# Weight conversion in three program stages instead of two, and the feature tiles of the scores' PSUM place first

## The chip, the cores and the metric

The kernel runs on one core of one Trainium2 chip. The metric is the device time of one execution in microseconds (us). The kernel before takes 1092.17 us, the median of three runs (1091.16 to 1093.48).

## The reference

An attention over chunks of 64 tokens feeds an FNet block. Batch 8, 8 heads, 576 tokens, head size 64, so the model size is 512; the feed-forward width is 2048.

```python
scores = scale * q_c @ k_c.T          # per batch, head and chunk of 64 tokens
attn   = softmax(scores)
x      = (attn @ v_c) -> (8, 576, 512)
u      = x + real(fft(fft(x, axis=1), axis=2))
un     = (u - mean(u)) / sqrt(var(u) + 1e-6)
out    = u + relu(un @ w_ch1) @ w_ch2
```

The two weights arrive as 64-bit floats. The kernel turns them into 32-bit floats itself, and that conversion is what the change is about.

## The kernel before

**Groups and sides.** Tokens are gathered in tiles of 128 rows. Group g of the feed-forward layer holds four such tiles (512 columns); group 0 belongs to batch 0, group 1 to batch 1, and so on. While TensorE multiplies for group g, the attention and the Fourier mix of batch g + 1, called its side, are worked in between. The main loop (lines 1213 to 1247) takes one step of `mlp(g)`, counts it in `t`, and then emits as many steps of the side as are due (`t0`, `t1`, `due`, lines 1218 to 1220). The order is written out by hand: under `manual_schedule` each engine, and the queue of the DMA issues on SyncE (SPq), works its instructions in the order in which the program emits them.

**Group 0.** `up_first` (line 943) has four blocks of four feature tiles (f = 0, 4, 8, 12) and four steps kk in each; step (f, kk) needs weight piece f + kk of `w_ch1`. A step is 8 matmul records of 128x512. At the end of a block ScalarE evicts four tiles (lines 962 and 965). The sixteen steps m of `down_plain` (line 988) follow; step m needs piece 16 + m, a slice of `w_ch2`. The first block's four tiles, `first_ups`, are two tiles of the pool `ps_f` and two halves of the one buffer of `ps_a` (tag "att"). The attention scores `sc` (line 379) and the attention outputs use this same `ps_a` buffer.

**Weight pieces.** There are 32 pieces of 128x512 numbers (`pieces`, line 266), 512 KB each as they arrive. `round_weight(i)` does for piece i the head h(i): two VectorE instructions that cut out the fraction and the exponent (lines 308 and 311); then the three ScalarE activations a(i) (lines 300, 303 and 306); and then the tail t(i - 1) of the piece before: three VectorE instructions (lines 321 to 323) that put the number together. One call is thus h(i), a(i), t(i - 1). Calls are made by `round_next`, once or twice in a step of the main loop (lines 1229 to 1231), none in a step in which the side did heavy VectorE work.

**Landing places.** A piece lands in one of seven spaces (`spaces`, line 138; numbered 0 to 6). A tail gives its space back and lets `load_weight` (line 279) issue the next load. Pieces from 8 on may use spaces 0 to 4 only (`N_EARLY`, `N_LATE`); pieces from 26 on (`N_LAST`) may use 2, 3 and 4 only, since spaces 0 and 1 are wanted by `keep2`, which prepares `w_ch2` for the later groups on VectorE once all pieces are converted.

**The side of batch 1.** `attention` (line 569) and `fourier` (line 644). The steps that the prediction names: T(n) transposes q and k of the side's tile n and issues the loads of the next tile; S(n) is the scores and, on VectorE, the maximum and the difference (lines 397 and 399), then the exponential on ScalarE; P(n) transposes the probabilities (`pT`, line 416); V(n) multiplies with v and divides on VectorE (lines 454 to 456). V(2) and V(3) also fold the tiles on VectorE (lines 491 to 529): these are the heavy steps. T(4) is the first tile of batch 2 and is transposed on VectorE (line 352). Then come z (line 652), its copies on ScalarE (lines 677 to 688), and three `mix` steps (line 700), each followed by VectorE (lines 710, 711, 717, 637). The normalised tile `un` (line 843) of group 1 needs the last of these.

Of the kernel before, what the change touches and what calls it, by code (L numbers as in the profile page):

```python
# [10 lines left out]
ACTF = mybir.ActivationFunctionType  # L11
# [5 lines left out]
def kernel(  # L17
# [32 lines left out]
    nc = tc.nc  # L50
# [9 lines left out]
    KD = DM // 128  # L60
    KF = DFF // 128
# [194 lines left out]
    def turn_dim_tables():  # L256
# [9 lines left out]
    pieces = [  # L266
        (w1[:, kk, f:f + 512], w_ch1[kk * 128:(kk + 1) * 128, f:f + 512])
        for f in range(0, DFF, 512)
        for kk in range(KD)
    ] + [(w2[:, m, :], w_ch2[m * 128:(m + 1) * 128, :]) for m in range(KF)]  # L270

    power = {}

    raws, free = {}, list(range(len(spaces)))

# [11 lines left out]
    def round_weight(i, later=None, parts="ht"):  # L287

        if "h" in parts and i < len(pieces):
            w, t = pieces[i][0], raw(i)
            lo, hi, wi = t[:, :, 0], t[:, :, 1], w.bitcast(U32)
            p = power[i] = three_p.tile([128, 512], U32, tag="o", name="power")

            def fraction(w=w, wi=wi):
                nc.scalar.activation(out=w, in_=wi, func=ACTF.Copy, scale=2.0 ** -20, bias=1.0)  # L300

            def exponent(p=p):
                nc.scalar.activation(out=p, in_=p, func=ACTF.Relu, scale=-1.0, bias=top[:, 0:1])

            def power_(p=p):
                nc.scalar.activation(out=p, in_=p, func=ACTF.Relu, scale=-8.0, bias=top[:, 1:2])

            nc.vector.tensor_scalar(wi, hi, 0x000FFFFF, None, ALU.bitwise_and)
            if later is None:
                fraction()  # L310
            nc.vector.tensor_scalar(p, hi, 0x7FF00000, None, ALU.bitwise_and)
            if later is None:
                exponent()
                power_()
            else:
                later += [fraction, exponent, power_]
        if "t" in parts and 0 < i <= len(pieces):
            w, t = pieces[i - 1][0], raw(i - 1)
            lo, hi = t[:, :, 0], t[:, :, 1]
            p = power.pop(i - 1)  # L320
            nc.vector.scalar_tensor_tensor(w, lo, 2.0 ** -52, w, ALU.mult, ALU.add)
            nc.vector.scalar_tensor_tensor(p, hi, 0x80000000, p, ALU.bitwise_and, ALU.bitwise_or)
            nc.vector.tensor_tensor(out=w, in0=w, in1=p.bitcast(FP32), op=ALU.mult)
            r = raws.pop(i - 1)
            if i - 1 + len(spaces) < N_EARLY or r < N_LATE:
                free.append(r)
            load_weight(max(raws, default=i - 1) + 1)
# [203 lines left out]
    def attention_early():  # L531

        lo, hi = first[0], first[1] - 1

        def ready(n):
            if n == at[LO, 0, 1]:
                shift_early(0)
            if n == at[HI, 0, 1]:
                fold(0, 1)
            if n == at[HI, 0, 0]:  # L540
                fold(0, 0)
            if n + 3 > hi:
                load_v(n + 3)

        att_T(lo)
        att_S(lo)
        for n in range(lo, hi + 1):
            if n < hi:
                att_T(n + 1)
            softmax(n)  # L550
            if n > lo:
                att_V(n - 1)
                ready(n - 1)
            if n < hi:
                att_S(n + 1)
            if n in (lo, hi):
                keep_warm(1)
            att_P(n)
        shift_early(1)
        fold(0, NM)  # L560
        keep_warm(1)
        att_V(hi)
        ready(hi)
        keep_warm(6)
        turn_tables()
        round_weight(0)
        round_weight(1, parts="t")

    def attention(b):

# [156 lines left out]
    def fourier_early():  # L727
# [53 lines left out]
        keep_warm(3)  # L781
        yield
        ups = ps_a.tile([128, 2, 512], FP32, tag="att", name="up_a")
        first_ups.extend([ps_f.tile([128, 512], FP32, tag="ff", name="up") for _ in range(2)])
        first_ups.extend([ups[:, i] for i in range(2)])

        def columns(s):

# [154 lines left out]
    def up_first():  # L943

        unT = unTs.pop(0)
        h1 = one_p.tile([128, KF, G * 128], FP32, tag="big", name="h1")
        for f in range(0, KF, 4):
            ups = first_ups if f == 0 else [ps_f.tile([128, G * 128], FP32, tag="ff", name="up") for _ in range(4)]  # L950
            for kk in range(KD):
                for m, up in enumerate(ups, f) if f + kk > 0 else ():
                    nc.tensor.matmul(  # L953
                        out=up,
                        lhsT=w1[:, kk, m * 128:(m + 1) * 128],
                        rhs=unT[:, kk],
                        start=(kk == 0),
                        stop=(kk == KD - 1),
                        skip_group_check=True,
                    )  # L960
                    if kk == KD - 1 and (f > 0 or m < 2):
                        nc.scalar.activation(out=h1[:, m], in_=up, func=ACTF.Relu)  # L962
                if kk == KD - 1 and f == 0:
                    for m in (2, 3):
                        nc.scalar.activation(out=h1[:, m], in_=ups[m], func=ACTF.Relu)
                yield h1

    def up_plain(g):
# [19 lines left out]
    def down_plain(g, h1):  # L988

        dns = [ps_f.tile([128, 512], FP32, tag="ff", name="dn") for _ in groups[g]]
        for m in range(KF):
            for s, dn in enumerate(dns):
                nc.tensor.matmul(  # L995
                    out=dn,
                    lhsT=h1[:, m, s * 128:(s + 1) * 128],
                    rhs=w2[:, m, :],
                    start=(m == 0),
                    stop=(m == KF - 1),  # L1000
                )
                if m == KF - 1:
                    n = groups[g][s]
                    if s < G - 1:
                        o = three_p.tile([128, DM], FP32, tag="o", name="o")
                    else:
                        o = one_p.tile([128, 2 * (HM + 1)], FP32, tag="two", name="o")[:, 0:DM]
                    nc.vector.tensor_tensor(out=o, in0=dn, in1=natural(n), op=ALU.add)
                    store(n, o)
            for j in range(G):  # L1010
                due = KF - (G - j + 1)
                if m == due - 2:
                    normed(g + 1, j)
                if m == due:
                    turned(g + 1, j)
                    if j >= 2 and g + 1 >= first_of[1]:
                        combined(g + 1, j - 2)
            yield
# [121 lines left out]
    with tc.manual_schedule():  # L1140
# [20 lines left out]
        n_w = 2  # L1161
# [8 lines left out]
        put_off, first_ups = [], []  # L1170

        def round_next(later=None):
            nonlocal n_w
            if n_w <= len(pieces):
                round_weight(n_w, later)
                n_w += 1

        keep_warm(8)
        attention_early()
# [32 lines left out]
        t = 0  # L1212
        for g in range(NG):
            for _ in mlp(g):
                t += 1
                heavy = False
                if cur < len(sides):
                    t0 = 2 if cur == 0 else ready_at[cur - 1]
                    t1 = ready_at[cur]
                    due = min(sizes[cur], (t - t0) * sizes[cur] // (t1 - t0))  # L1220
                    while done < due:
                        heavy = next(sides[cur], None) or heavy
                        done += 1
                    if t >= t1:
                        for _ in sides[cur]:
                            pass
                        cur, done = cur + 1, 0
                if not heavy:
                    round_next()
                    if t <= 1 or t < KF and t % 4 == 0 or t >= KF + 3:  # L1230
                        round_next()

                if n_w > len(pieces) and t >= KF + 7:
                    for _ in range(3):
                        next(conv2, None)
                if t == begin[1] - 1:
                    for _ in conv2:
                        pass
                if begin[1] <= t < begin[1] + KF // 2:
                    for _ in range(3):  # L1240
                        next(conv1, None)
                if t == begin[1] + KF // 2:
                    for _ in range(NS2):
                        fetch(2)
                if t == begin[1] + KF:
                    for _ in range(NS1):
                        fetch(1)
# [49 lines left out]
```

## Time and profile before

| what | value |
|---|---|
| time, median of 3 | 1092.17 us |
| span of the profiled execution | 1090.8 us |
| TensorE busy (modelled) | 1069.5 us |
| VectorE busy | 576.9 us |
| ScalarE busy | 298.8 us |
| mean granted TensorE clock | 0.999 |
| group 0, up and down | about 46 to 190 us of the span |
| conversion of pieces 2 to 31 | about 48 to 156.5 us of the span |

Busy time is a sum over the whole span. The stage of the change is only a seventh of it, so the views to read are those that can be cut to a stretch: the busy time by stretch, the timeline of one engine (start, duration, instruction, and in brackets the idle time before it with what ended it), and the chain that ended last in order of time.

### The profile page before, as it was taken

To read this page: it belongs to the slowest core of one execution; us is meant where nothing else is said; L and a number is where in the kernel's file an instruction comes from. 1 tells how busy PE (TensorE), PEld (TensorE's weight loads), DVE (VectorE), ACT (ScalarE), POOL (GpSimd) and SP (SyncE) were. 2 spreads that over 40 slices of the span, in tenths; PEclk is the share of its full clock that TensorE was granted. 3 is DMA by queue.
4 is the path that set the end of the run, shared out by engine and by line. 5 is a ranking of instruction groups with operands and counts; after the bars stand their busy time and mean duration, and the time that the engine had idled before them with its cause. 6 is when DMAs were issued, how large, how long until landed. Compare 5 with 4: busy or idle time off the path is not lost.

```text
span 1090.8 us, 18838 instructions
## 1 busy us (share of the span) xinstructions
PE 1069.5 (98%) x7018; PEld 848.3 (78%) x7018; DVE 576.9 (53%) x1258; ACT 298.8 (27%) x730; POOL 281.4 (26%) x403
## 2 busy tenths in 40 slices
PE   8999999999999999999999999999999999999998
PEld 6644454447888888888888888888888888888887
DVE  4889997214566355663556455735663534323411
ACT  4777553222112310322022212321133103101300
POOL 4300002344405240254024220514051401220140
PEclk9999999999999999999999999999999999999999
DMA  8767656679575637692668457754653455446232
GB/s 170 243 168 180 174 169 227 176 239 307 177 204 165 198 135 205 196 263 89 197 170 228 140 169 221 203 175 150 198 184 89 143 196 160 122 154 210 78 116 78
DMA packets 147970, 192.73 MB, mean 177 GB/s; under 512 B 66126, under 2 KB 104014, under 8 KB 140712
## 3 DMA queue, kind: packets, MB, share of 16 engines
q1 hardware_dynamic: 145620, 190.20, 58.1%
q8 instruction: 56, 0.92, 0.4%
q0 software_dynamic: 512, 0.68, 0.3%
q10 hardware_dynamic: 1748, 0.66, 0.2%
q14 instruction: 34, 0.28, 0.1%
HBM read 167.22 MB, written 24.12 MB: 175 GB/s over the span
## 4 chain that ended last, share of the span: by engine, by line
PE 85%; DVE 5%; DMA 3%; ACT 3%; SPq 2%; issue 1%; POOL 0%; DVEq 0%; ACTq 0%; POOLq 0%
PE pb L1090 20%; PE pa L1041 17%; PE pa L1090 15%; PE pb L1041 13%; PE pt L333 3%; PE up L974 3%; PE up L953 2%; DMA k<-in_k_dram 2%; PE more_z L652 2%; PE sc L384 2%; PE mix L700 2%; PE z L652 1%; PE xp L432 1%; PE dn L995 1%; PE idle L1168 1%; SPq L195 1%
## 5 line engine op out<-in xcount | busy, mean ns | idle before, releaser
L1041 PE MATMUL pa<-unT,wa 128*128 128x256 f32 x672 | 159.3, 380 | 0.0
L1041 PEld LDWEIGHTS pa<-unT,wa 128*128 128x128 f32 x672 | 126.6, 190 | 17.2
L941 POOL TENSOR_TENSOR h<-h 128x256 f32<-128x256 f32 x64 | 55.9, 880 | 267.4 <-PE pb L1041 150.5
L1090 PE MATMUL pa<-wb,h 128*128 128x256 f32 x512 | 115.6, 380 | 0.0
L1090 PE MATMUL pb<-wb,h 128*128 128x256 f32 x512 | 114.9, 379 | 0.0
L1041 PE MATMUL pb<-wa 128*128 128x256 f32 x448 | 106.7, 381 | 0.0
L1090 PEld LDWEIGHTS pa<-wb,h 128*128 128x128 f32 x512 | 96.1, 190 | 13.5 <-issue 0.5
L1090 PEld LDWEIGHTS pb<-wb,h 128*128 128x128 f32 x512 | 96.3, 190 | 12.6
L1041 PEld LDWEIGHTS pb<-wa 128*128 128x128 f32 x448 | 84.3, 190 | 11.7 <-DVE h L1060 0.2
L995 PE MATMUL dn<-wb,h 128*128 128x512 f32 x128 | 57.4, 596 | 1.3 <-ACT h L962 1.3
L1090 PE MATMUL pb<-wb,yall 128*128 128x256 f32 x256 | 58.2, 381 | 0.0
L1047 DVE TENSOR_TENSOR wa<-pb,wa 128x256 f32<-128x256 f32 x56 | 23.6, 424 | 65.4 <-ACT wa L1046 65.4
L1090 PE MATMUL pa<-wb,yall 128*128 128x256 f32 x256 | 57.9, 380 | 0.0
L1090 PE MATMUL pb<-wb 128*128 128x256 f32 x256 | 57.7, 379 | 0.0
L974 PE MATMUL up<-unT,wa 128*128 128x512 f32 x128 | 56.8, 595 | 0.0
L1046 ACT COPY wa<-pa 128x256 f32<-128x256 f32 x56 | 20.8, 372 | 124.9 <-PE pa L1041 124.9
L1041 PE MATMUL pb<-unT,wa 128*128 128x256 f32 x224 | 53.0, 379 | 1.3 <-DMA wa<-s 1.3
L717 POOL TENSOR_TENSOR xall<-y,xall 128x513 f32<-128x513 f32 x14 | 21.2, 1517 | 126.2 <-DVE y L711 126.2
L1041 PE MATMUL pa<-wa 128*128 128x256 f32 x224 | 53.5, 382 | 0.0
L1090 PEld LDWEIGHTS pa<-wb,yall 128*128 128x128 f32 x256 | 47.7, 190 | 6.4
L1090 PEld LDWEIGHTS pb<-wb,yall 128*128 128x128 f32 x256 | 47.7, 190 | 6.3
L1090 PEld LDWEIGHTS pb<-wb 128*128 128x128 f32 x256 | 47.6, 190 | 5.9
(250 smaller groups left out, 1684.1 us busy)
## 6 DMA issues: line engine op xcount, KB each, us to landing
wb<-s SPq DMA_DIRECT2D x56, 1024.0 KB
wa<-s SPq DMA_DIRECT2D x196, 256.0 KB
xall<-in_moe_w_ch_dram SPq DMA_DIRECT2D x22, 512.0 KB
q<-in_q_dram SPq DMA_DIRECT2D x96, 112.0 KB
k<-in_k_dram SPq DMA_DIRECT2D x96, 112.0 KB
v<-in_v_dram SPq DMA_DIRECT2D x124, 64.0 KB
yall<-in_moe_w_ch_dram SPq DMA_DIRECT2D x10, 512.0 KB
s<-wb SPq DMA_DIRECT2D x20, 256.0 KB
```

Source lines behind the costliest of these rows:

```text
L333: nc.tensor.transpose(pt[:, j, :], src(j), ident)
L384: nc.tensor.matmul(out=sc[t0:t0 + CH, e, j * CH:(j + 1) * CH], lhsT=a[r0:r0 + D, 2 * j + c, 0:CH], rhs=b[r0:r0 + D, 2 * j + c, 0:CH], star ...
L652: nc.tensor.matmul(out=out_, lhsT=lhsT[p], rhs=tk[p, i, T // 2 if T != 5 else 0, cols], start=start, stop=stop, skip_group_check=True,)
L700: nc.tensor.matmul(out=mix[:, cols], lhsT=zt[:, T], rhs=tab, start=(T == 0), stop=(T == 3), skip_group_check=True,)
L717: eng.tensor_tensor(out=x[:, 0:w], in0=y[:, 0:w], in1=x[:, 0:w], op=ALU.add)
L941: nc.gpsimd.tensor_tensor(out=h1[:, m, hi], in0=h1[:, m, lo], in1=h1[:, m, hi], op=ALU.subtract)
L953: nc.tensor.matmul(out=up, lhsT=w1[:, kk, m * 128:(m + 1) * 128], rhs=unT[:, kk], start=(kk == 0), stop=(kk == KD - 1), skip_group_check=True,
L974: nc.tensor.matmul(out=up, lhsT=w1[:, kk, m * 128:(m + 1) * 128], rhs=unT[:, kk], start=(kk == 0), stop=(kk == KD - 1),)
L995: nc.tensor.matmul(out=dn, lhsT=h1[:, m, s * 128:(s + 1) * 128], rhs=w2[:, m, :], start=(m == 0), stop=(m == KF - 1),)
L1041: nc.tensor.matmul(out=dst, lhsT=w[:, kk, r], rhs=rhs[o][:, kk], start=(o in (0, 1) and kk == 0), stop=(kk == 1), skip_group_check=True,)
L1047: nc.vector.tensor_tensor(out=b, in0=pbs[r][:, 0], in1=a, op=ALU.add)
L1090: nc.tensor.matmul(out=dst, lhsT=lhs[:, m], rhs=w[:, m], start=(o in (0, 2) and m == 0), stop=(m == HF - 1), skip_group_check=True,)
```

## The change

A call of `round_weight(i)` becomes h(i), a(i - 1), t(i - 2): the activations are put aside in `acts` and emitted in the next call, after the next head, and the tail comes one call later than before. The purpose is that VectorE, ScalarE and VectorE again each work on another piece, so that neither waits inside a call for what the other has just been given. There is one call more in all (`len(pieces) + 1`), `need(i)` makes sure that the tail of a piece is emitted ahead of the matmul that reads it, step t = 2 takes two calls, and the side of batch 1 begins a step later (`t0` = 3). Separately, `first_ups` lists the two `ps_a` tiles first, and they are evicted right after their last matmul, so that the scores can have the buffer sooner.

```diff
-    power = {}
+    power, acts = {}, {}
...
             nc.vector.tensor_scalar(wi, hi, 0x000FFFFF, None, ALU.bitwise_and)
-            if later is None:
-                fraction()
             nc.vector.tensor_scalar(p, hi, 0x7FF00000, None, ALU.bitwise_and)
             if later is None:
-                exponent()
-                power_()
+                acts[i] = [fraction, exponent, power_]
             else:
                 later += [fraction, exponent, power_]
+        for do in acts.pop(i - 1, ()):
+            do()
+        i -= 1
         if "t" in parts and 0 < i <= len(pieces):
             w, t = pieces[i - 1][0], raw(i - 1)
...
         round_weight(0)
-        round_weight(1, parts="t")
+        round_weight(1, parts="")
+        round_weight(2, parts="t")
...
         ups = ps_a.tile([128, 2, 512], FP32, tag="att", name="up_a")
+        first_ups.extend([ups[:, i] for i in range(2)])
         first_ups.extend([ps_f.tile([128, 512], FP32, tag="ff", name="up") for _ in range(2)])
-        first_ups.extend([ups[:, i] for i in range(2)])
...
             for kk in range(KD):
+                need(f + kk)
                 for m, up in enumerate(ups, f) if f + kk > 0 else ():
...
-                    if kk == KD - 1 and (f > 0 or m < 2):
-                        nc.scalar.activation(out=h1[:, m], in_=up, func=ACTF.Relu)
-                if kk == KD - 1 and f == 0:
-                    for m in (2, 3):
-                        nc.scalar.activation(out=h1[:, m], in_=ups[m], func=ACTF.Relu)
+
+                    if kk == KD - 1 and (f > 0 or m > 0):
+                        for m_ in (0, 1) if f == 0 and m == 1 else (m,):
+                            nc.scalar.activation(out=h1[:, m_], in_=ups[m_ - f], func=ACTF.Relu)
...
         for m in range(KF):
+            if g == 0:
+                need(KF + m)
...
-            if n_w <= len(pieces):
-                round_weight(n_w, later)
+            if n_w <= len(pieces) + 1:
+                if n_w > 2:
+                    round_weight(n_w, later)
+                else:
+                    round_weight(n_w, later, "h")
                 n_w += 1
+
+        def need(i):
+
+            while n_w < i + 3:
+                round_next()
...
-                    t0 = 2 if cur == 0 else ready_at[cur - 1]
+                    t0 = 3 if cur == 0 else ready_at[cur - 1]
...
-                    if t <= 1 or t < KF and t % 4 == 0 or t >= KF + 3:
+                    if t <= 2 or t < KF and t % 4 == 0 or t >= KF + 3:
                         round_next()
 
-                if n_w > len(pieces) and t >= KF + 7:
+                if n_w > len(pieces) + 1 and t >= KF + 7:
```

## The prediction

> **What bounds the kernel now.** First the page: TensorE is busy 1069.5 of 1090.8 us, so removed waits can bring at most a per cent or two, and new TensorE waits are paid in full. Busy time by stretch, cut to the change's stage (columns: TensorE, its weight loads, VectorE, ScalarE, GpSimd, clock, DMA share, GB/s):
>
> ```profile
> 60.00:70.00 10.00, 8.78 (x57) 4.37 (x56) 6.40 (x13) 7.20 (x13) 0.00 (x0) 1.00 0.31 79
> 130.00:150.00 20.00, 20.00 (x82) 10.21 (x82) 19.16 (x38) 14.70 (x24) 0.00 (x0) 1.00 0.44 116
> ```
>
> At 60 to 70 VectorE and TensorE both have holes; at 130 to 150 both are full. Next the timeline of TensorE, for its waits:
>
> ```profile
> 63.69 0.69 PE L384 MATMUL sc<-kT,qT 64*64 64x64 f32 x32 [1.22 <-issue]
> ...
> 116.45 3.70 PE L995 MATMUL dn<-wb,h 128*128 128x512 f32 x8 [1.32 <-ACT h L962]
> ...
> 159.43 0.46 PE L700 MATMUL mix<-ce,zf 128*128 128x129 f32 x2 [1.11 <-DVE y L711]
> ...
> 172.25 0.66 PE L333 MATMUL pt<-ident,un 128*128 128x128 f32 x4 [0.36 <-ACT un L843]
> ```
>
> The first is the scores' wait for the `ps_a` buffer: its last eviction ends at 63.58. The last two say that TensorE comes to group 1's `un` with only 0.36 us of waiting: up to there VectorE and TensorE are nearly level. So I read the chain of waits and the timelines of VectorE and SPq:
>
> ```profile
> 135.51 0.61 DVE power L322
> 136.14 3.62 DMA xall<-in_moe_w_ch_dram
> 139.76 0.02 issue
> 139.78 0.43 DVE wb L308
> ```
>
> ```profile
> 97.95 4.21 SPq L195 DMA_DIRECT2D q<-in_q_dram  x8
> 102.25 4.96 SPq L195 DMA_DIRECT2D k<-in_k_dram  x8
> 107.31 0.37 SPq L285 DMA_DIRECT2D xall<-in_moe_w_ch_dram  x1
> ...
> 136.14 11.52 SPq L285 DMA_DIRECT2D xall<-in_moe_w_ch_dram  x5
> ```
>
> ```profile
> 64.44 0.69 DVE L397 TENSOR_REDUCE mx<-sc 128x8 f32<-128x512 f32 x1 [3.50 <-PE sc L384]
> ...
> 139.78 0.43 DVE L308 TENSOR_SCALAR wb<-xall 128x512 uint32<-128x512 uint32 x1 [0.34 <-DMA xall<-in_moe_w_ch_dram]
> ```
>
> From 129 to 172 the chain is mostly VectorE's weight calls, with loads between them: a piece's load, issued as the tail's second instruction ends, lands 3.62 us later, and the next head starts at once. The last SPq line is loads 27 to 31, the five that have only three spaces: they already cost 0.34, 0.22 and 0.97 us (timeline, heads 27, 29, 31).
>
> **What the Trainium skill says.** "TensorE: Matmul & The Clock Gate", Architectural detail, calls ScalarE's and VectorE's queues strict FIFO. The trace agrees: VectorE idles 3.50 us for the scores at 64.44 while the next head's data lies ready. "DMA: Bandwidth & Descriptors", Anatomy of one DMA, says that waits are taken by the issuing sequencer before dispatch, and gives about 2.0 us + bytes/436 GB/s for the software path; an estimate for 512 KB is 3.2 us. Here 3.62 was measured on SPq, and I use that. The clock page's Part 1 halves the clock after an idle window of about 3.4 us and restores it after a busy one. No wait of this trace is that long after the start (mean clock 0.999), so nothing here tests it.
>
> **Edit 1, `ps_a` first.** It lets the scores' buffer go after the second of the four last matmuls; with the side a step later, T(0) and block f = 4 start without the wait: -1.22 us. Other small waits ahead of T(3) (0.23 us at 81.39, others as small) add some 0.9, since ScalarE no longer sits behind a just-cut head when evictions fall due. T(3), at 97.31 now, comes at about 95.1. Adding the TensorE items from 62.3 by their durations (a step 3.44, a T 0.87, S 0.67, P 0.44, V 0.63) gives the same.
>
> **Edit 2, the three stages.** It adds no instruction. A call is 2.60 us on VectorE (heads at 131.55 and 134.15): head 0.67, tail 1.93. ScalarE's three take 1.9 (129.40 to 131.31). It removes VectorE's waits for them, 2.2 us in four (waits list). At the start head 3 slips ahead of tail 1, which then ends near 51.2 instead of 50.5; its matmul starts at 51.12 now, so 0.1 at most.
>
> **Edit 2 and the loads.** This is the term that decides. Written out from the code, call 25 before is h25, a25, t24, and t24 issues load 27; call 26 follows, and then h27: 0.65 + 2.60 us for a load of 3.62. After, t24 is in call 26 (h26, a25, t24), and h27 is **the very next VectorE instruction**. With three spaces and a piece in three stages, load i can only go out in tail i - 3, which stands directly ahead of head i. The head could start 0.65 us after the issue (136.76 for 136.11 now), the data come at 3.62 + 0.02: a wait of 3.0 us. It recurs for heads 27 to 31, as each load waits for a tail behind the last wait: 5 x 3.0 = 15.1 us. The load that fed h26, and the ones before with five spaces, go out three calls ahead and land in time, save one.
>
> That one is load 21. It stands on SPq behind T(3)'s 16 q and k loads, which take 0.64 + 9.36 us from T(3)'s start (97.31 to 107.31 now). With T(3) at 95.1, load 21 goes at 105.1 and lands at 108.7. VectorE asks for it earlier than now, since h21 moves from after S(3) and T(4) to before both: S(2)'s scores end at 91.8, + 1.33 (maximum, difference), + call 17 (2.60), + calls 18 and 19 (5.20) and 0.75 for ScalarE behind the evictions, + V(1) 1.04, + call 20 (2.60) = 105.4. Wait: 3.3 us.
>
> **What it does to the end of group 0.** From 108.7: call 21 2.60, S(3) 1.33, exponential and a21 on ScalarE 2.6, first eviction 0.6: down step 0 starts at 115.85 (116.45 now), so the gain of edit 1 is spent. Then 3.44 + 0.65 and V(2)'s VectorE work begins at 120.05. Now it begins at 116.06, ahead of step 0. P(3) and V(3) now fall into one step: TensorE waits about 0.7 us for the copy of `pT` (as at 25.27, 0.73 after P), hidden since VectorE is in V(2)'s fold for 6.35 (116.06 to 122.41).
>
> VectorE from V(2) to the last tail: V(2) 6.35, V(3) 3.94 (125.01 to 128.95), calls 24 to 31 8 x 2.60 = 20.8, five waits 15.1, two bare tails 3.86: 50.05 us. Now the stretch is 116.06 to 156.48, 40.4. The last tail thus ends at 170.1 instead of 156.5: **+13.6 us**.
>
> **Who waits behind it.** VectorE's `keep2`, `mix` and statistics work is FIFO behind these tails and leads to `un` by the same 14.9 us chain (156.48 to 171.38), so TensorE's transpose at 172.25 moves by the same 13.6. ScalarE's a30 waits for h30 at 158.1, and the copies of z are queued behind a30: the first `mix` can start only near 161.3. TensorE gets there at about 151.6: it **idles some 9.7 us**, and again about 5 at the third `mix`. If the clock halves there, the re-warming after the third `mix` lies on the path: 0 to 3.4 us (one or two windows at half speed), less the 0.36. I take 1.0. Everything later is emitted relative to these steps and moves with them.
>
> Sum: 1092.2 + 13.6 + 1.0 = **1106.8 us**.
>
> **The rivals.** (a) Load 21 is in time (its issue, or T(3), earlier than I put it). Then step 0 starts at 112.95, V(2) at 117.1, and the shift is 10.6: 1102.8. For it: the three-microsecond difference rests on a sum of some twenty terms; against it: 9.36 us of issue are read directly. Chance 0.2. (b) The clock: both idle stretches leave TensorE at half speed for two windows, 3.0 in place of 1.0, and queues behind the late loads add a microsecond: 1110. For it: 9.7 us is far over the page's window; against it: the first cold spell is absorbed by the second wait. Chance 0.1. (c) **Faster**: the ring's waits stay hidden, because VectorE comes so late that tails and loads have slack, and only the early gains count: 1.22 + 0.9 + 0.3 = 2.4, giving 1089.8. For it: VectorE's waits for ScalarE and TensorE's for evictions are real. Against it: h27 follows t24 with nothing between, whatever the hour. Chance 0.06. (d) Evened out, within 0.2%: gains and half-hidden waits cancel, 1092. Chance 0.02.
>
> My forecast has 0.62. The range leaves out (c) and (d) and part of (b): 1101 to 1110. Slower 0.92, same 0.02, faster 0.06.
>
> **What would show it.** In the profile after: on SPq, loads 27 to 31 one by one, 5.6 us apart, where five now go in 11.5 us; VectorE's heads 27 to 31 with about 3 us each for the DMA, in all near 15; a wait of about 3 at h21; no 1.22 at the scores and no 3.50 on VectorE; TensorE idle for several us ahead of the first `mix` and again of the third, and the clock below 1 after them, if the page applies; the last tail near 170. I am wrong if heads 27 to 31 wait under 1 us each, or if TensorE's transposes of `un` don't move with the last tail.

## The result and the profile after

The changed kernel takes **1107.74 us** (1107.54 to 1112.51, 4 runs) against 1091.66 us for the kernel before (1089.94 to 1093.48): a ratio of **1.0157**, 95% interval 1.0125 to 1.019. It is 1.6% slower; 1106.8 was predicted, with a range of 1101 to 1110.

Page, slices of 27.6 us (tenths busy; PEclk is the granted TensorE clock): counted from 0, TensorE's busy share dips in slices 4 to 6 (111 to 193 us) and its granted clock in slices 5 and 6 (138 to 193 us), and neither does after that.

```profile
PE   7999868999999999999999999999999999999998
...
PEclk9999988999999999999999999999999999999999
```

Timeline of TensorE, start and duration in us, in brackets the idle time before and what ended it:

```profile
116.91 5.37 PE L999 MATMUL dn<-wb,h 128*128 128x512 f32 x8 [3.82 <-ACT h L967]
...
127.65 0.70 PE L433 MATMUL xp<-v,pT 64*64 64x65 f32 x32 [0.68 <-ACT pT L417]
...
163.60 0.80 PE L702 MATMUL mix<-ce,zr 128*128 128x129 f32 x2 [8.59 <-ACT zr L683]
...
176.29 0.46 PE L702 MATMUL mix<-ce,zf 128*128 128x129 f32 x2 [2.45 <-DVE y L713]
...
177.46 7.03 PE L999 MATMUL dn<-wb,h 128*128 128x512 f32 x16
...
189.11 0.66 PE L334 MATMUL pt<-ident,un 128*128 128x128 f32 x4 [0.36 <-ACT un L845]
```

The 1.22 us ahead of the scores is gone from the list. In its place stand 3.82 us ahead of the first down step, 8.59 ahead of the first `mix` and 2.45 ahead of the third. The 7.03 us at 177.46 are compared with another kernel's further down. The last line answers to 172.25 before, again with 0.36 us of waiting: group 1's `un` comes 16.9 us later. Timeline of VectorE over the same stretch:

```profile
109.80 0.43 DVE L309 TENSOR_SCALAR wb<-xall 128x512 uint32<-128x512 uint32 x1 [3.45 <-DMA xall<-in_moe_w_ch_dram]
...
123.03 0.17 DVE L455 TENSOR_SCALAR rd<-xp 128x8 f32<-128x8 f32 x1 [2.16 <-PE xp L433]
...
144.21 0.43 DVE L309 TENSOR_SCALAR wb<-xall 128x512 uint32<-128x512 uint32 x1 [2.95 <-DMA xall<-in_moe_w_ch_dram]
...
149.73 0.43 DVE L309 TENSOR_SCALAR wb<-xall 128x512 uint32<-128x512 uint32 x1 [2.83 <-DMA xall<-in_moe_w_ch_dram]
...
155.19 0.43 DVE L309 TENSOR_SCALAR wb<-xall 128x512 uint32<-128x512 uint32 x1 [2.77 <-DMA xall<-in_moe_w_ch_dram]
...
160.64 0.43 DVE L309 TENSOR_SCALAR wb<-xall 128x512 uint32<-128x512 uint32 x1 [2.75 <-DMA xall<-in_moe_w_ch_dram]
...
166.88 0.43 DVE L309 TENSOR_SCALAR wb<-xall 128x512 uint32<-128x512 uint32 x1 [3.55 <-DMA xall<-in_moe_w_ch_dram]
```

The first line is head 21, the second V(2); the last five are heads 27 to 31, 14.85 us of waiting in all. VectorE's 3.50 us for the first tile's scores are gone, but it now waits 3.18 us for the second tile's, at 79.23. SPq and the chain of waits show why:

```profile
96.52 4.25 SPq L195 DMA_DIRECT2D q<-in_q_dram  x8
100.87 5.06 SPq L195 DMA_DIRECT2D k<-in_k_dram  x8
106.03 0.37 SPq L285 DMA_DIRECT2D xall<-in_moe_w_ch_dram  x1
...
140.55 22.40 SPq L285 DMA_DIRECT2D xall<-in_moe_w_ch_dram  x5
```

```profile
139.92 0.61 DVE power L323
140.54 0.02 issue
140.55 3.63 DMA xall<-in_moe_w_ch_dram
144.18 0.02 issue
144.21 0.43 DVE wb L309
```

Load 21 goes out at 106.03, behind the sixteen q and k issues. The five last loads stretch over 22.4 us of SPq where they took 11.5, and each link of the chain is the same: second tail instruction, load, head. The five landings take 3.63, 3.51, 3.44, 3.43 and 4.22 us; behind the last one, load 31, a store goes out 0.4 us later (163.01).

A measure that runs through the experiments is the **stage**: the time from TensorE's first transposition of `un` in group 0 to the first in group 1. Before it is 172.25 - 43.91 = 128.34 us, after 189.11 - 43.88 = 145.23. It leaves out the start, which moves by up to 4.3 us between profiles, and the 915 to 918.6 us after the stage, which scatter as well. It comes from one profile of each kernel, and a single wait in it can vary: head 21 waited 3.45, 3.43 and 4.82 us in three profiles (the changed kernel, a_last28 and a_five) whose programs are the same up to there. The ratios come from many runs.

### The profile page after: what moved, and what is told of

Read it like the earlier page. It is cut to its first block, busy times and chain, and to the rows that moved or that the text cites. A ratio compares the mean times of both kernels' runs of the same rounds, so it can differ in the third digit from the quotient of the medians.

```text
span 1105.7 us, 18836 instructions
## 1 busy us (share of the span) xinstructions
PE 1073.2 (97%) x7018; PEld 849.8 (77%) x7018; DVE 576.9 (52%) x1258; ACT 298.7 (27%) x730; POOL 281.6 (25%) x403
## 4 chain that ended last, share of the span: by engine, by line
PE 83%; DVE 6%; DMA 5%; SPq 2%; ACT 2%; POOL 1%; issue 1%; DVEq 0%; POOLq 0%; ACTq 0%
PE pb L1094 20%; PE pa L1045 17%; PE pa L1094 15%; PE pb L1045 12%; PE up L976 3%; PE pt L334 3%; PE up L956 3%; DMA xall<-in_moe_w_ch_dram 2%; PE dn L999 2%; DMA k<-in_k_dram 2%; PE more_z L654 2%; PE mix L702 1%; PE sc L385 1%; PE z L654 1%; PE xp L433 1%; SPq L195 1%
## 5 line engine op out<-in xcount | busy, mean ns | idle before, releaser
L1094 PEld LDWEIGHTS pa<-wb,h 128*128 128x128 f32 x512 | 96.1, 190 | 13.5 <-issue 0.4
L999 PE MATMUL dn<-wb,h 128*128 128x512 f32 x128 | 61.5, 631 | 3.8 <-ACT h L967 3.8
```

Of the source, the lines that this page charges most:

```text
L999: nc.tensor.matmul(out=dn, lhsT=h1[:, m, s * 128:(s + 1) * 128], rhs=w2[:, m, :], start=(m == 0), stop=(m == KF - 1),)
L1094: nc.tensor.matmul(out=dst, lhsT=lhs[:, m], rhs=w[:, m], start=(o in (0, 2) and m == 0), stop=(m == HF - 1), skip_group_check=True,)
```

## The experiments

All ratios are to the kernel before on the same chip, with 95% intervals.

| kernel | ratio | stage, us | against 128.34 |
|---|---|---|---|
| changed | 1.0157 (1.0125 to 1.019) | 145.23 | +16.89 |
| a_five: changed, five spaces to the end | 1.0022 (1.0008 to 1.0035) | 131.31 | +2.97 |
| a_load: changed, load 21 ahead of q and k | 1.0132 (1.0118 to 1.0146) | 142.79 | +14.45 |
| a_five_load: both | 0.9976 (0.9969 to 0.9983) | 127.48 | -0.86 |
| b_two: before, two spaces at the end | 1.0122 (1.0108 to 1.0136) | 141.62 | +13.28 |
| a_side2: changed, side at the old step | 1.0121 (1.0103 to 1.014) | 143.56 | +15.22 |
| a_last28: changed, limit from piece 28 | 1.0052 (1.0036 to 1.0067) | 135.28 | +6.94 |
| b_psa: before, first edit alone | 0.9985 (0.9978 to 0.9992) | 127.33 | -1.01 |
| b_five: before, five spaces to the end | 0.9981 (0.9975 to 0.9988) | 127.56 | -0.78 |
| b_psa_five: before, both of these | 0.9982 (0.9974 to 0.9989) | 126.51 | -1.83 |
| b_psa_five_pool: the same, k loads on GpSimd's queue | 0.9974 (0.9966 to 0.9983) | 126.53 | -1.81 |
| a_five_pool: changed, five spaces, k loads on GpSimd's queue | 0.9983 (0.9975 to 0.999) | 126.75 | -1.59 |
| a_five_pool_side2: the same, side at the old step | 0.9972 (0.9962 to 0.9981) | 124.88 | -3.46 |

**Is it the ring of three spaces?** Two kernels ask it from both sides. The first gives the changed kernel all five spaces to the end:

```diff
-    N_LATE, N_EARLY, N_LAST = 5, 8, 26
+    N_LATE, N_EARLY, N_LAST = 5, 8, 40
```

> The changed kernel with all five spaces for pieces 26 to 31 (N_LAST 40 in place of 26); nothing else is altered. Ring theory: the five waits of heads 27 to 31 (14.9 us in the changed kernel) fall under 0.5 us in all, since each load then goes out three calls ahead; the last tail comes near 158.5 in place of 173.3, the wait for load 21 (3.45) stays, and the time is 1092 to 1094.5. Rival, the side's later step and the folding of P(3) and V(3) into one step (not the ring) costs the time: it stays at 1105 to 1108.

The time, 1095.35 us, is a little above the expectation, far below the rival's. The ring's five waits are gone from VectorE's list, and 13.9 of the 16.9 us with them. What is left is head 21, which in this profile waited longer still (4.82 us), and the first down step behind it:

```profile
119.93 5.40 PE L999 MATMUL dn<-wb,h 128*128 128x512 f32 x8 [5.18 <-ACT h L967]
...
176.86 0.66 PE L334 MATMUL pt<-ident,un 128*128 128x128 f32 x4 [0.35 <-ACT un L845]
```

The second takes the kernel before, with its two stages, and gives its last pieces two spaces, so that there too a load can only go out in the tail right ahead of its head:

```diff
-        fit = [r for r in free if (i < N_EARLY or r < N_LATE) and (i < N_LAST or r > 1)]
+        fit = [r for r in free if (i < N_EARLY or r < N_LATE) and (i < N_LAST or r > 2)]
```

> The kernel before (two stages) with two spaces in place of three for pieces 26 to 31. Ring theory: a load can then only go out in the tail that stands directly ahead of its head, as in the changed kernel, so heads 27 to 31 wait about 3.0 us each, 15 in all (1.5 in the kernel before), TensorE idles several us ahead of the first mix, and the time is 1104 to 1106. Rival, the three stages themselves or the side's step cost the time: the two-stage kernel hides the shorter ring, 1092 to 1095.

It takes 1105.59 us, inside the expectation. VectorE's list of waits (total, times, longest) and TensorE's:

```profile
DVE wb L308 <- DMA xall<-in_moe_w_ch_dram: 15.0, 5, 3.6
```

```profile
PE mix L700 <- ACT zr L681: 10.6, 1, 10.6
```

Neither the third stage nor the side's later step is in this kernel. What it shares with the changed kernel is that spaces minus stages is zero, and its stage grows by 13.28 us of the changed kernel's 16.89: 15.0 less the 1.5 that heads 27, 29 and 31 waited already is 13.5.

**How far does it depend on the lead?** The limit is set from piece 28 on:

```diff
-    N_LATE, N_EARLY, N_LAST = 5, 8, 26
+    N_LATE, N_EARLY, N_LAST = 5, 8, 28
```

> The changed kernel with N_LAST 28 in place of 26, so that load 27 may take a space that came free three calls earlier and loads 28 to 31 then go out one whole call before their head. Ring theory by lead: 0.65 + 2.60 us of lead against 3.6 of landing leaves some 0.4 us at heads 28 to 31 in place of 2.8 to 3.6, under 2 us in all; the wait for load 21 stays; time 1093 to 1096. Rival, the number of pieces bound to three spaces counts and not the lead: four of the five waits stay, 1102 to 1104.

The total, 1097.39 us, lies above what I expected, and the picture differs from mine:

```profile
135.18 0.35 SPq L285 DMA_DIRECT2D yall<-in_moe_w_ch_dram  x1
140.39 11.29 SPq L285 DMA_DIRECT2D xall<-in_moe_w_ch_dram  x4
```

```profile
155.63 0.43 DVE L309 TENSOR_SCALAR wb<-xall 128x512 uint32<-128x512 uint32 x1 [3.58 <-DMA xall<-in_moe_w_ch_dram]
```

One head waits, not four a little. With load 27 in `yall` (space 0), loads 28, 29 and 30 go out one call ahead, and their heads come without a wait that the view shows. But tail 27 gives back space 0, which load 31 may not use; load 31 has to wait for tail 28, which stands directly ahead of head 31: 3.58 us again. I had counted the lead as the same for all. The rule holds piece by piece, and the total of the waits follows it, 14.85, 3.58 and 0 (changed, a_last28, a_five); the rival, waits by the number of bound pieces, does not. Another part of the overshoot is the clock: TensorE waited 4.54 us ahead of the third `mix`, ran at half clock behind it, and came to group 1's `un` 16.9 us after the last tail, not 15.8.

**The wait for load 21.** The q and k loads of batch 2's first tile, which T(3) issues, are put behind the first weight call of their step:

```diff
-        if first[1] <= n + 1 < NT:
+        if n + 1 == first[2]:
+            waiting.append(n + 1)
+        elif first[1] <= n + 1 < NT:
             load(n + 1)
...
                     round_next()
+                    while waiting:
+                        load(waiting.pop())
```

> The changed kernel with the q and k loads of tile 4's successor put behind the first weight call of their step, so that load 21 goes out ahead of those 16 issues; the three spaces stay. Theory: the 3.45 us wait of head 21 and most of the 3.82 us wait of the first down step go, with the cold clock behind it (8 records in 5.4 us in place of 3.4); the five ring waits stay near 14.9. Time 1102 to 1104.5. Rival, that wait is hidden by the ring's: no change, 1107 to 1108.

The time, 1106.4 us, is above the expectation, and its interval overlaps that of the changed kernel; the stage is 2.4 us shorter. Head 21 no longer waits, but a part of its wait passes to head 22, whose load is now the one behind q and k:

```profile
DVE wb L310 <- DMA xall<-in_moe_w_ch_dram: 15.1, 5, 3.5
...
DVE wb L310 <- DMA yall<-in_moe_w_ch_dram: 1.1, 1, 1.1
```

The first line is the ring, untouched; the second is head 22. Counted from the start of the stage, V(2) begins 3.8 us sooner than in the changed kernel and the last tail ends 3.6 us sooner, about what the theory said. A third of this is lost behind the third `mix`:

```profile
172.31 0.46 PE L705 MATMUL mix<-ce,zf 128*128 128x129 f32 x2 [2.77 <-DVE y L716]
...
173.48 8.73 PE L1002 MATMUL dn<-wb,h 128*128 128x512 f32 x16
```

The same 16 records take 7.03 us in the changed kernel, after a wait of 2.45. Here the granted clock falls to half behind the wait (0.50 from 174 to 177 us), and `un` comes 16.9 us after the last tail, not 15.8. Both repairs together:

> Both repairs in the changed kernel: five spaces to the end, and load 21 ahead of the 16 q and k issues. Theory: nothing of the loss is left and the gains of the first edit show: the last tail near 152.7 (156.5 before the change), time 1087.5 to 1089.5, faster than both kernels. Rival, the later side (V(2) behind the first down step, P(3) with V(3)) costs something of its own: 1091 to 1094.

1090.03 us, 0.24% under the kernel before, but not as low as expected: with the ring out of the way, head 22 waits 2.58 us. The third stage, `need` and the side's later step are all still in it, so none of these by itself makes the loss. Added up, the two repairs alone take 13.92 + 2.44 = 16.4 us off the stage, together 17.8 (a_load alone pays the clock behind the third `mix`): the loss is accounted for by the two waits and what hangs on them.

**Is it the side's later step?**

```diff
-                    t0 = 3 if cur == 0 else ready_at[cur - 1]
+                    t0 = 2 if cur == 0 else ready_at[cur - 1]
```

> The changed kernel with the side of batch 1 begun at the old step (t0 = 2). Ring theory: the five waits stay near 15 us and the time with them, 1104 to 1108. Rival, the later side costs the time: 1092 to 1096.

1105.15 us: the loss stays, and the rival falls. The later step does cost something, though: head 21 waits 1.94 instead of 3.45, the 3.82 us ahead of the first down step are not there, and the stage is 1.7 us shorter. The last tail ends 2.8 us sooner in the stage; as in a_load, the wait ahead of the third `mix` (2.82 us) is followed by half clock, and 1.2 us go there.

**What are the edits worth without the waits?** The first edit alone in the kernel before:

```diff
+        first_ups.extend([ups[:, i] for i in range(2)])
         first_ups.extend([ps_f.tile([128, 512], FP32, tag="ff", name="up") for _ in range(2)])
-        first_ups.extend([ups[:, i] for i in range(2)])
...
-                    if kk == KD - 1 and (f > 0 or m < 2):
-                        nc.scalar.activation(out=h1[:, m], in_=up, func=ACTF.Relu)
-                if kk == KD - 1 and f == 0:
-                    for m in (2, 3):
-                        nc.scalar.activation(out=h1[:, m], in_=ups[m], func=ACTF.Relu)
+                    if kk == KD - 1 and (f > 0 or m > 0):
+                        for m_ in (0, 1) if f == 0 and m == 1 else (m,):
+                            nc.scalar.activation(out=h1[:, m_], in_=ups[m_ - f], func=ACTF.Relu)
```

> The kernel before with the first edit alone: the two feature tiles in the scores' PSUM place come first and are evicted after the second matmul. Theory: the scores' wait of 1.22 us falls to about 0.1 and VectorE's of 3.50 to about 2.4, worth about 1.1 us at the end since VectorE's chain begins there: 1090 to 1091. Rival, the wait is hidden by VectorE's later chain: under 0.3 us.

1090.33 us, a ratio of 0.9985. The scores' wait is 0.20 where it was 1.22, and the stage is shorter by just this 1.0 us:

```profile
66.25 0.70 PE L384 MATMUL sc<-kT,qT 64*64 64x64 f32 x32 [0.20 <-issue]
```

The other half of the ring's question, five spaces in the kernel before (the same line as in a_five), and both of these together:

> The kernel before with five spaces for pieces 26 to 31. Ring theory: the three waits of heads 27, 29 and 31 (0.34, 0.22 and 0.97 us) go, worth 0.5 to 1.5 us: 1090 to 1091. Rival, these waits are beside TensorE's own work there: no change within 0.3.

> The kernel before with the first edit and five spaces: two stages, the ring mended. Theory: the two gains add, 1088.5 to 1090. If it equals the changed kernel with both repairs, the third stage itself is worth nothing; the theory gives the third stage VectorE's waits for ScalarE (2.2 us in the kernel before), so this one should be 0.5 to 2 us slower than that.

1089.51 us, half a microsecond under the expectation, and 1089.81 us. In the stage the gains add (-1.01, -0.78, together -1.83); in the whole time b_psa_five is not told apart from either, since the rest of the program scatters by more than that. Nor is it slower than a_five_load by the 0.5 to 2 us expected: their intervals overlap, and its stage is 1.0 us shorter. That comparison does not price the third stage, since a_five_load still has head 22's wait in it.

**What is the third stage worth?** The last three kernels move the k loads of that one tile to GpSimd's queue, so that SPq comes to load 21 sooner:

```diff
-        for src, dst, nm, eng in ((q, qs, "q", nc.sync), (k, ks, "k", nc.scalar if n == 0 else nc.sync)):
+        for src, dst, nm, eng in (
+            (q, qs, "q", nc.sync),
+            (k, ks, "k", nc.scalar if n == 0 else nc.gpsimd if n == first[2] else nc.sync),
+        ):
```

> The changed kernel with five spaces to the end and the k loads of batch 2's first tile (8 of the 16 issues ahead of load 21) issued on GpSimd's queue in place of SPq; the engines' own order is unaltered. Theory, the place in SPq delays loads 21 and 22: both go about 5 us sooner, heads 21 and 22 wait under 0.5 us, the stage from the first transposition of un of group 0 to that of group 1 takes 125 to 126 us (128.3 before the change, 131.3 with five spaces alone), time 1088 to 1089.5. Rival, the transfers of q and k themselves fill the DMA engines: the wait stays above 2 us.

> The same move of the k loads in the two-stage kernel with the first edit and five spaces. Its heads never waited for load 21, so nothing is to be had: the stage stays at 126.5 us within 0.4, and the time at 1089 to 1090.5. If the three-stage kernel above is the faster one by 0.7 to 1.5 us, that is what the third stage is worth once its loads are in time; if they are equal, it is worth nothing.

> As the first of these, with the side begun at the old step (t0 = 2), so that V(2) comes ahead of the first down step and P(3) and V(3) are a step apart again. Theory: TensorE's wait for the copy of pT (0.7) goes; VectorE gets the side's work earlier, and the stage takes 125 to 127 us, within 1 us of the kernel with t0 = 3.

The expectation of the first failed: head 21 still waits 1.96 us, and the stage is 126.75 us, not 125 to 126.

```profile
102.58 0.37 SPq L285 DMA_DIRECT2D xall<-in_moe_w_ch_dram  x1
```

```profile
109.28 0.43 DVE L309 TENSOR_SCALAR wb<-xall 128x512 uint32<-128x512 uint32 x1 [1.96 <-DMA xall<-in_moe_w_ch_dram]
```

Load 21 goes out at 102.58, but its head starts only at 109.28: 6.7 us after the issue, against 109.80 - 106.03 = 3.8 in the changed kernel. The eight k loads, issued on GpSimd's queue from 98.19 to 102.43, took a median of 6.2 us to land, so some of them were still moving when load 21 went out; the mean DMA share between its issue and its head is 1.06 here and 0.87 there. So the place in the queue was a part of the cause. That the transfers themselves are the rest fits these figures, but no run takes the two apart.

With t0 = 3, three stages (126.75) and two (126.53) come out even, head 21 still waiting. With t0 = 2 no head waits for a load any more, and three stages take 124.88 us of stage, 1.65 less than two and 1.87 less than with t0 = 3, where at most 1 was expected. VectorE's lists of waits, from the start of the stage to the last tail, bear the 1.65 out: for the scores 3.7 us with two stages and 3.2 with three, for ScalarE's part of the weight calls 2.7 and 1.5. In the whole time that is 0.9972 against 0.9974: not told apart. a_five_pool_side2, at 1088.65 us, is the lowest of all and beats both kernels, but with its 0.28% it can't be called better than the two-stage kernel with the same repairs.

## Why the prediction was right, and where its steps were off

**The ring held to the fraction of a microsecond.** Five waits of 3.0, 15.1 in all, were forecast; 2.95, 2.83, 2.77, 2.75 and 3.55 came, 14.85. The last is the longest: load 31 landed in 4.22 us, not in 3.62. From V(2) to the last tail 50.05 was forecast; 123.03 to 173.34 is 50.3. And `un` follows the last tail as said: 189.11 - 173.34 = 15.8, as 172.25 - 156.48 = 15.8 before.

**Load 21** was forecast to be asked for at 105.4 and to land at 108.7; it was asked for near 106.35 and the head began at 109.80. The wait of 3.3 was 3.45. T(3) came at 95.89 where I had 95.1: the "others as small" of edit 1 were 0.8 us too generous. The place is right. That its removal would bring 3 to 6 us in the time, as I then expected of a_load, was wrong: 3.6 us came as far as the last tail, and the clock behind the third `mix` took 1.2 of them back.

**Edit 2 removed less than I put.** Of the 2.2 us that VectorE waited for ScalarE ahead of the tails, 1.4 are still in its list of waits after the change.

**The clock was the mis-placed term.** I allowed 1.0 us behind the third `mix`. There TensorE was at full clock (1.00 from 172 to 178 us). The cost lay where I had put none: at the first down step, after 3.82 us of waiting, where 8 records took 5.37 us in place of 3.44. V(2) waits for exactly these (the 2.16 us at 123.03). The forecast's own times, 115.85 for this step and 112.95 with load 21 in time, less 0.6 for the eviction, put a wait of 3.5 us there; I did not ask what the clock would do. The granted clock by stretch (columns as in the prediction):

```profile
117.00:122.00 5.00, 5.00 (x8) 1.99 (x8) 3.83 (x7) 3.17 (x6) 0.00 (x0) 0.67 0.87 238
...
163.00:168.00 5.00, 3.88 (x10) 2.89 (x11) 1.45 (x4) 3.50 (x21) 0.00 (x0) 0.50 0.56 157
```

This is what the Trainium skill, "TensorE: Matmul & The Clock Gate", Part 1, describes: half clock after an idle window of about 3.4 us. The trace before could not test it; here 3.82 and 8.59 us of idling were each followed by it. As a limit, 3.4 us does not hold here: in a_load and a_side2, 2.77 and 2.82 us were enough. In this stage of the 14 profiles every wait of TensorE of 2.77 us or more was followed by half clock, and none of 2.45 us or less.

In the changed kernel the second spell cost nothing: the down step behind the first `mix` took 5.94 us, and TensorE waited 2.45 us for VectorE after it all the same, in place of the 5 forecast. It was a near thing: in a_load, where this wait was 2.77 us, half clock followed and took 1.2 us, just where I had allowed 1.0. b_two agrees on the second spell: 10.6 us of idling, its clock halved too, and VectorE's waits alone account for the loss.

**The sum.** V(2) at 123.03 and not 120.05: about 1.1 from T(3) and load 21, 1.9 from the clock. So `un` moved by 16.9, not 13.6 + 1.0: the forecast was 2.3 us low in the stage. The median moved by only 1107.74 - 1091.66 = 16.1, and in the two profiles 2 us came back after the stage (918.6 to 916.6). Other kernels show 915 to 918 there; why is not settled. That the total is met to 0.9 us is thus in part luck: of the 2.3 us, 0.8 came back outside the stage, and the kernel before measured 0.5 us less than the 1092.2 that the sum began with. Two sums of the working are off by a tenth: h21 is asked for at 105.3 and V(2) begins at 119.9 by their own terms. Rival (a)'s 1102.8 leaves out the 1.0 for the clock.

**The rivals.** (a), load 21 in time, is not what happened; (b) was right that the clock would cost more than 1.0, but it cost 1.9 and not 3.0, and in another place; (c), waits that stay hidden, is refuted by each of the five lines. That the side's step or the third stage by itself costs the time is refuted by a_side2, b_two and a_five_load.

## What to carry to other kernels

A stage more in a pipeline holds each buffer one turn longer: count the buffers of the shortest ring it runs over, not of the usual one. Here five spaces would have done, and the last five pieces had three; one load's landing of 3.6 us then stood in every turn. And when a wait is removed from a shared in-order queue, ask who stands next in it: here a part of the wait only passed on to the next load. Then ask what a removed wait starts behind it: in a_load a later wait of TensorE grew from 2.45 to 2.77 us, and a third of the gain went into the clock behind it.

## What was not expected of the hardware

Idle spells of 2.77, 2.82 and 3.82 us were enough to halve TensorE's clock for the microseconds behind them, and one of 2.45 us was not. In the changed kernel the clock was 0.50 in every half microsecond from 117 to 120 and 1.00 from 120.5 on, so that the wait of 3.82 us cost 1.9 us more than itself. And a 512 KB load that landed in 3.4 to 3.6 us while little else moved (mean DMA share 0.41 to 0.51, loads 27 to 30 of the changed kernel) took 6.7 us in a_five_pool, with k loads of 56 KB each still moving (share 1.06).
